# Attention and experts on one core: GpSimd's remainders of k and q as steps of their own, and a new written order

## The chip, the core and the metric

One core of a Trainium2 chip runs the whole program. The metric is the device time of one execution in microseconds (us). Three runs of the kernel before gave 1462.18, 1463.23 and 1466.3 us; the median, 1463.23 us, is the time to beat.

TensorE (PE) multiplies matrices, VectorE (DVE) and ScalarE (ACT) work on elements, GpSimd (POOL) does element work and gathers, SyncE (SP) issues transfers.

## What is computed

Attention over 8 batches and 8 heads of 576 positions with head dimension 64, where of each row of scores only those within tau of the row's maximum are kept; then a mixture of 8 experts with the best two of each token.

```python
scores = scale * np.matmul(q, k.transpose(0, 1, 3, 2))
thresh = np.max(scores, axis=-1, keepdims=True) - tau
scores = np.where(scores >= thresh, scores, -1000000000.0)
scores = scores - np.max(scores, axis=-1, keepdims=True)
attn = np.exp(scores)
attn = attn / (np.sum(attn, axis=-1, keepdims=True) + 1e-09)
return np.matmul(attn, v)
...
logits = x @ w_gate
noisy_logits = logits + np.log1p(np.exp(x @ w_noise)) * noise
top2 = np.argpartition(-noisy_logits, 2, axis=1)[:, :2]
...
h = np.maximum(x[mask] @ w1[e], 0.0)
out[mask] += top2_w[mask, k, None] * (h @ w2[e])
```

## The kernel before

The 64 pairs of batch and head are worked in 32 pairs of heads, n = 0 to 31 (four to a batch). Each pair has nine tiles of scores, j = 0 to 8, of 128 rows by 576 columns. For each tile PE computes the scores into PSUM (`scores`, L257 and, for j = 0, L262), DVE scales them into `ns` and takes the row's maximum (`rowmax`, L275), ACT computes `e` = exp (L277) and, once for two tiles, a threshold `thr` (L281), and DVE keeps what lies above it (`mask`, L303, one instruction with the two SBUF inputs ns and e). Then PE turns the masked tile (`ptile`, L320, L331, L334; `prem`, L348), ACT copies the result out of PSUM (L323, L337, L338, L351), PE multiplies with v (`avpiece`, `avrem`, L374), ACT copies the output (`oev`, L401), PE turns it for the gate (`xlpart`), and DVE scales it into `xr` (`xev`, L430 and L432), after `norm` (L361) and `invert` (L365, L366).

Scores are exact to float32 by three products of split operands. SP loads q and k of a pair in one transfer of 640 KB (`load`, L196, two buffers). `split_k` and `split_q` each let ACT round 128x640 elements to the short format (`hik`, `hiq`, L208) and then POOL compute the remainder (`lok`, `loq`, L209, 128x640, which reads the loaded tile and the rounded one in SBUF). hi and lo have two buffers each. Pair 0 uses the loaded values unsplit.

The order on every engine is written out by hand. `attention()` lists every step with a number, `at(g + t, step, n, ...)`, where g = 9n and t comes from the table PAIR (LAST for pair 31, NEXT for pair 30); the steps are sorted by that number and then issued, each to its engines. So a pair's steps reach over about two stretches of nine: in the steady state the last masks of one pair stand between the first steps of the next. An engine does its instructions in that order, and each waits until its inputs and buffers are ready.

Between these stand the steps of the gate of each finished batch (`gate_...`, small operations on DVE, ACT and POOL, and `gate_put`, L659 and L660, which POOL issues), and, from pair 30 on, the first steps of the experts: weights split by ACT and POOL (L838, L839), rows gathered by POOL (L886) and turned by DVE (L922) and POOL (L925). When attention is over, the experts run to the end of the program.

Of the kernel before, what the change touches and what calls it, by code (L numbers as in the profile page):

```python
# [10 lines left out]
F32 = mybir.dt.float32  # L11
# [5 lines left out]
ALU = mybir.AluOpType  # L17
# [37 lines left out]

NEXT = dict(
    scores=(-0.03, 1.15, 2.25, 3.09, 4.96), rowmax=(0.96, 1.61, 1.83, 2.74, 3.02, 3.28, 4.69, 5.12, 5.53),
    mask=(1.71, 2.04, 2.18, 4.54, 4.88, 5.36, 5.88, 5.87, 6.39), ptile=(7.71, 5.72, 7.01, 6.48, 7.05), prem=(8.49,),
    norm=(12.67,), invert=(15.81,), avrem=(10.66,), avpiece=(12.13, 13.04, 13.04, 13.69, 8.64, 8.65, 8.66, 11.21),
    oev=(14.72, 12.07), xlpart=(15.86, 15.72), xev=(16.20, 16.59))  # L60

MLAG = 2

# [10 lines left out]
    raw=(-19, -19, -9), tok=-27, ix=-24.5, ga=(-24, -22, -20), ba=(-22, -20, -18), la=(-20, -17, -15), ta=(-11, -10, -7),  # L74
# [78 lines left out]
def attention(tc, const, work, psum, state, qk, v, tau, wgn, noise, noise_r, out, x_dram, table, experts):  # L153
    nc = tc.nc
# [10 lines left out]
    def done(key):  # L165
        idle.append(used.pop(key))
# [14 lines left out]
    some, scale = (const.tile([128, 1], F32, name=x) for x in ("some", "scale"))  # L181
# [9 lines left out]
    raw = {}  # L191
# [36 lines left out]
    st = {}  # L228
# [61 lines left out]
    def mask(n, j):  # L290
        ns, thr, e = st.pop((n, j))
        t, s = tile_of(j)
        if j == 0:
            ssum[n] = rot(work, [128, 10], F32, name="ssum", bufs=3)
            pr = st["w", n] = rot(work, [128, S + 64], F32, name="pr")
            if n < 2:
                nc.vector.memset(pr[:, S:], 0.0)
            st["p", n, 8] = pr[:, None, 0:S]
        if s == 0:
            st["p", n, t] = P[:, next(turn) % 6]  # L300
        p = st["p", n, t][:, place(t, s) if j else 0, :]
# [102 lines left out]
    xr, xlp = {}, {}  # L404
# [38 lines left out]
    vec, gp = nc.vector, nc.gpsimd  # L443
# [225 lines left out]
    def at(g, f, *a):  # L669
        ev.append((g, len(ev), f, a))  # L670
# [10 lines left out]
    for n in range(NP):  # L681
        g = 9 * n
        d = dict(PAIR, **(LAST if n == NP - 1 else NEXT if n == NP - 2 else {}))
        for f in (scores, rowmax, mask):
            for i, t in enumerate(d[f.__name__]):
                at(g + t, f, n, 2 * i - 1 if f is scores and i else i)
        for i, t in enumerate(d["ptile"]):
            at(g + t, ptile, n, (i - 1) % 5)
        for f in (prem, norm, invert, avrem):
            at(g + d[f.__name__][0], f, n)  # L690
        for i, t in enumerate(d["avpiece"]):
            at(g + t, avpiece, n, i // 4, i % 4)
# [38 lines left out]
class Experts:  # L731
# [509 lines left out]
```

## Time and profile before

| | |
|---|---|
| median of three runs | 1463.23 us |
| profiled execution | 1465.06 us, of which the span in the trace 1463.2 us |
| PE busy | 1377.6 us (94%) |
| DVE busy | 918.8 us (63%) |
| ACT busy | 686.7 us (47%) |
| POOL busy | 598.1 us (41%) |

The times of the trace start with its span; the 1.86 us that the profiled execution took beside the span lie outside it. The shares are means over the whole program. Attention takes the span from 0 to about 600 us, the experts the rest, and the two have different limits, so each stretch is to be read by itself.

### The profile page before, as it was taken

Reading aid. Unit: us, or ns where it says so; the run is one execution under the profiler, and the core shown is the slowest. Engines: PE = TensorE matmul, PEld = TensorE weight load, DVE = VectorE, ACT = ScalarE, POOL = GpSimd, SP = SyncE. Lnnn points to the kernel's source line nnn. Section 1 sums busy time; section 2 is a strip of 40 time slices with the busy share of each in tenths; the row PEclk is TensorE's granted clock in tenths of the full one; section 3 lists DMA queues with packets and bytes.
Section 4 is the critical chain, followed back from the end, with each engine's and each line's share of the span. In section 5 each row is a group of like instructions: output and inputs, shape, how many; then the busy total and the mean of one; then the engine's idle time right before and its main releaser. Section 6 shows DMA issues by size and latency. Waiting matters only on the chain. (4 is left out here: it accounts for less than half of the span.)

```text
span 1463.2 us, 29503 instructions
## 1 busy us (share of the span) xinstructions
PE 1377.6 (94%) x11034; PEld 1166.2 (80%) x11034; DVE 918.8 (63%) x2558; ACT 686.7 (47%) x1447; POOL 598.1 (41%) x757
## 2 busy tenths in 40 slices
PE   8999999999999887889999999999999999999995
PEld 6667666766676555778988999999999989989884
DVE  8999999999999786453544444454454543543410
ACT  6888889898988776232222132232222221221210
POOL 2135555464746545533162262352432522521612
PEclk7999999999999887899999999999999999999998
DMA  5133425242414044455466376386375474573422
GB/s 174 61 110 91 136 85 147 67 135 67 135 45 124 21 121 119 81 132 107 149 151 158 80 167 153 87 183 152 83 186 136 115 169 110 133 172 83 69 30 32
DMA packets 154130, 166.55 MB, mean 114 GB/s; under 512 B 58148, under 2 KB 105340, under 8 KB 152960
## 3 DMA queue, kind: packets, MB, share of 16 engines
q1 hardware_dynamic: 126784, 125.21, 29.3%
q0 software_dynamic: 27200, 39.42, 16.2%
q8 instruction: 87, 1.43, 0.4%
q14 instruction: 59, 0.48, 0.1%
HBM read 104.42 MB, written 60.15 MB: 112 GB/s over the span
## 5 line engine op out<-in xcount | busy, mean ns | idle before, releaser
L303 DVE SCALAR_TENSOR_TENSOR p<-ns,thr,e 128x576 f32<-128x576 f32 x256 | 252.7, 1017 | 2.9 <-ACT thr L281 1.5
L277 ACT ACTIVATE e<-ns,nm 128x576 f32<-128x576 f32 x288 | 212.2, 779 | 45.3 <-DVE ns L275 44.4
L275 DVE TENSOR_SCALAR_CACHE_REDUCE ns<-sp 128x576 f32<-128x576 f32 x279 | 200.1, 746 | 31.7 <-PE sp L262 17.6
L374 PE MATMUL tp<-pt,vt 128*64 128x256 f32 (+1 forms) x1024 | 154.6, 435 | 1.2 <-ACT pt L323 0.9
L982 POOL DMA_INDIRECT out<-m_y,sx x43 | 68.1, 1585 | 206.9 <-DVE m_y L963 171.5
L257 PE MATMUL sp<-hik,hiq 64*128 64x288 f32 x496 | 124.0, 367 | 29.7 <-DVE ns L275 28.7
L982 POOL DMA_INDIRECT out<-m_y,ix x54 | 87.8, 1626 | 150.7 <-DVE m_y L1021 137.9
L323 ACT ACTIVATE pt<-tp 128x512 f32<-128x512 f32 x256 | 135.4, 596 | 24.9 <-PE tp L320 20.8
L963 DVE TENSOR_SCALAR m_y<-m_sp,gw 128x512 f32<-128x512 f32 (+1 forms) x43 | 32.3, 751 | 162.6 <-PE m_sp L961 162.6
L942 ACT ACTIVATE m_p<-m_tp 128x384 fp32r<-128x384 f32 (+1 forms) x66 | 32.6, 494 | 210.7 <-PE m_tp L940 210.6
L209 POOL TENSOR_TENSOR lok<-kq,hik 128x640 fp32r<-128x640 f32 x31 | 51.7, 1668 | 183.9 <-ACT hik L208 183.9
L257 PEld LDWEIGHTS sp<-hik,hiq 64*128 64x128 f32 x496 | 75.1, 207 | 56.3 <-DVE ns L275 51.0
L320 PE MATMUL tp<-ident,p 64*128 64x64 f32 x2048 | 107.2, 253 | 12.8 <-DVE xr L432 5.6
L320 PEld LDWEIGHTS tp<-ident,p 64*128 64x128 f32 x2048 | 98.4, 164 | 23.3 <-PE sp L257 10.3
L374 PEld LDWEIGHTS tp<-pt,vt 128*64 128x64 f32 x1024 | 67.5, 143 | 57.5 <-issue 24.1
L886 POOL DMA_INDIRECT m_p<-x_rows,sx x71 | 69.8, 983 | 92.7 <-DMA stage<-m_p 60.2
L257 PE MATMUL sp<-lok,hiq 64*128 64x288 f32 x496 | 104.6, 328 | 0.0
L660 POOL DMA_INDIRECT slot_table<-pay,sl x80 | 89.5, 1119 | 24.5 <-issue 12.7
L257 PE MATMUL sp<-hik,loq 64*128 64x288 f32 x496 | 98.6, 314 | 0.0
L942 ACT ACTIVATE m_hik<-m_tp 128x384 fp32r<-128x384 f32 (+1 forms) x11 | 5.6, 506 | 187.4 <-PE m_tp L940 187.4
L257 PEld LDWEIGHTS sp<-hik,loq 64*128 64x128 f32 x496 | 73.1, 209 | 0.0
L940 PE MATMUL m_tp<-m_pt,m_pt 128*128 128x384 f32 (+1 forms) x396 | 72.1, 340 | 0.0
(384 smaller groups left out, 3616.4 us busy)
## 6 DMA issues: line engine op xcount, KB each, us to landing
m_kq<-w SPq DMA_DIRECT2D x128, 256.0 KB
kq<-qk SPq DMA_DIRECT2D x32, 640.0 KB
stage<-m_p SPq DMA_DIRECT2D x63, 256.0 KB
vt<-v SPq DMA_DIRECT2D x8, 1280.0 KB
out<-zeros SPq DMA_DIRECT2D x19, 512.0 KB
x_rows<-xr SPq DMA_DIRECT2D x32, 256.0 KB
m_zeros<-stage SPq DMA_DIRECT2D x96, 64.0 KB
m_vt<-stage SPq DMA_DIRECT2D x96, 64.0 KB
```

Of the source, the lines that this page charges most:

```text
L209: nc.gpsimd.tensor_tensor(lo, x, hi.bitcast(F32), op=ALU.subtract)
L257: nc.tensor.matmul(sp[s][:, hh, 0:HALF], q_[p, 128 * t:128 * t + 128], k_[p, k0:k0 + HALF], start=(i == 0), stop=(i == last))
L275: nc.vector.tensor_scalar(ns, sp[:, :, 0:HALF], -1.0 / math.sqrt(D) if n else scale, None, op0=ALU.mult, op1=ALU.min, accum_out=nm)
L277: nc.scalar.activation(e, ns, AF.Exp, bias=nm, scale=-1.0)
L303: nc.vector.scalar_tensor_tensor(p, ns, thr, e, op0=ALU.is_le, op1=ALU.mult, accum_out=ssum[n][:, c:c + 1])
L320: nc.tensor.transpose(tp[a][:, 4 * s + kt, :], p[r, 128 * kt:128 * kt + 128], ident[r, r])
L323: nc.scalar.activation(pt[n][:, :, :, c:c + 64].rearrange("p s k c -> p (s k) c"), tp[a], AF.Copy)
L374: nc.tensor.matmul(av[n, i][64 * s:64 * s + 64, 0:PIECES[i][1] - PIECES[i][0]], w, x, start=(k == 1), stop=(k == 5))
L660: st = nc.gpsimd.indirect_dma_start(out=table, out_offset=bass.IndirectOffsetOnAxis(ap=d["sl"][0:m, i, c:c + 1], axis=0), in_=d["pay"][0:m ...
L886: self.nc.gpsimd.indirect_dma_start(out=r[0:m], out_offset=None, in_=x, in_offset=bass.IndirectOffsetOnAxis(ap=self.tok[e][2][0:m, t:t + 1 ...
L940: nc.tensor.matmul(ps[:, 0:n], w[:, 128 * c:128 * c + 128], x[:, c, 0:n], start=(i == 0), stop=(i == len(ops) - 1))
L982: st = self.nc.gpsimd.indirect_dma_start(out=out, out_offset=bass.IndirectOffsetOnAxis(ap=idx, axis=0), in_=y, in_offset=None, compute_op= ...
```

## The change

`split_k` and `split_q` now hold ACT's rounding alone. The subtraction on POOL is a step of its own, `split_rest`, with its own number in the table (`rest_k`, `rest_q`), and it gets a dependency on the DVE instruction (rowmax, mask or xev) that was issued last before it. All three tables have new numbers. `load(2)` moves from 5.54 to 8.76, and the puts of the last batches but one (`put0`) lie later and closer together. The same arithmetic is done as before.

```diff
 PAIR = dict(
-    scores=(-0.03, 1.15, 2.44, 3.28, 5.50), rowmax=(0.96, 1.91, 1.92, 3.22, 3.26, 4.63, 5.00, 7.40, 7.41),
+    scores=(1.09, 1.57, 2.27, 4.41, 8.72), rowmax=(1.45, 1.72, 1.82, 3.28, 3.30, 6.19, 7.12, 9.93, 10.27),
...
-    xev=(20.09, 20.43), split_q=(-9.93,), split_k=(-10.40,))
+    xev=(21.41, 21.02), split_q=(-9.01,), split_k=(-4.23,), rest_q=(-3.85,), rest_k=(-4.11,))
...
         nc.scalar.activation(hi, x, AF.Copy, scale=some)
-        nc.gpsimd.tensor_tensor(lo, x, hi.bitcast(F32), op=ALU.subtract)
         st[name, n] = hi, lo
+        st["raw", name, n] = x
+
+    def split_rest(n, name):
+
+        hi, lo = st[name, n]
+        sub = nc.gpsimd.tensor_tensor(lo, st.pop(("raw", name, n)), hi.bitcast(F32), op=ALU.subtract)
+        if "vec" in st:
+            tc.add_manual_dep(sub.ins, st["vec"].ins.name,
+                              mybir.DependencyInfo(mybir.DependencyClass.Sync, mybir.DependencyReason.DATA),
+                              reason="starts behind the last mask")
...
         if n + 2 < NP:
-            at(g - 3 if n else 5.54, load, n + 2)
+            at(g - 3 if n else 8.76, load, n + 2)
         if n:
...
+            at(g + (d["rest_q"][0] if n > 2 else max(d["rest_q"][0], -9.58)), split_rest, n, "q")
+            at(g + d["rest_k"][0], split_rest, n, "k")
```

**In the middle of the program.** GpSimd, in the fifth batch, before; lok and loq are the remainders, kq the loaded tile, L660 a put.

```order
L659 MEMSET spacer 1x1 [waits Pool_49]
L660 DMA slot_table<-pay_6334,sl_6342 37152x2
L209 TENSOR_TENSOR lok_6672<-kq_6340,hik_6671 128x640 [waits DMAHW5_49,PE_49,Activation_49]
L659 MEMSET spacer 1x1 [waits Pool_49]
L660 DMA slot_table<-pay_6334,sl_6342 37152x2
L209 TENSOR_TENSOR loq_6679<-kq_6340,hiq_6678 128x640 [waits PE_49,Activation_49]
L659 MEMSET spacer 1x1 [waits Pool_49]
```

VectorE at the same place before (ns to the right of the arrow: a mask; ns to its left: a row maximum; the numbers of tiles rise in the order of issue, so the step with hik_6671 was issued between the row maxima of ns_6664 and ns_6699):

```order
L275 TENSOR_SCALAR ns_6658,nm_6659<-sp_6613 128x576
L275 TENSOR_SCALAR ns_6664,nm_6659<-sp_6614 128x576
L303 SCALAR_TENSOR_TENSOR p,ssum_6472<-ns_6585,thr_6587,e_6589 128x576
L303 SCALAR_TENSOR_TENSOR p,ssum_6472<-ns_6593,thr_6587,e_6595 128x576
L275 TENSOR_SCALAR ns_6699,nm_6700<-sp_6682 128x576
L303 SCALAR_TENSOR_TENSOR p,ssum_6472<-ns_6658,thr_6660,e_6662 128x576
L303 SCALAR_TENSOR_TENSOR p,ssum_6472<-ns_6664,thr_6660,e_6666 128x576
L275 TENSOR_SCALAR ns_6764,nm_6765<-sp_6706 128x576
L275 TENSOR_SCALAR ns_6770,nm_6765<-sp_6707 128x576
L303 SCALAR_TENSOR_TENSOR pr_6779,ssum_6778<-ns_6699,thr_6701,e_6703 128x576
L430 TENSOR_TENSOR xr_120<-tp_6740,ssum_6141 128x4x80
L432 TENSOR_TENSOR xr_120<-tp_6740,ssum_6141 64x80
```

GpSimd after:

```order
L669 MEMSET spacer 1x1 [waits Pool_49]
L670 DMA slot_table<-pay_6301,sl_6310 37152x2
L217 TENSOR_TENSOR lok_6583<-kq_5947,hik_6582 128x640 [waits DVE_49,DMAHW3_49,PE_49,Activation_49]
L217 TENSOR_TENSOR loq_6356<-kq_5947,hiq_6355 128x640 [waits PE_49]
L669 MEMSET spacer 1x1 [waits Pool_49]
L670 DMA slot_table<-pay_6301,sl_6310 37152x2
```

VectorE after; the masks of ns_6485 and ns_6491 are the pair's second and third, and the remainders wait for the second:

```order
L313 SCALAR_TENSOR_TENSOR p,ssum_6519<-ns_6485,thr_6487,e_6489 128x576
L313 SCALAR_TENSOR_TENSOR p,ssum_6519<-ns_6491,thr_6487,e_6493 128x576
L285 TENSOR_SCALAR ns_6604,nm_6605<-sp_6568 128x576
L285 TENSOR_SCALAR ns_6615,nm_6605<-sp_6569 128x576
L313 SCALAR_TENSOR_TENSOR p,ssum_6519<-ns_6547,thr_6549,e_6551 128x576
L313 SCALAR_TENSOR_TENSOR p,ssum_6519<-ns_6553,thr_6549,e_6555 128x576
L313 SCALAR_TENSOR_TENSOR p,ssum_6519<-ns_6604,thr_6606,e_6608 128x576
L285 TENSOR_SCALAR ns_6672,nm_6673<-sp_6641 128x576
L285 TENSOR_SCALAR ns_6686,nm_6673<-sp_6642 128x576
L375 RECIPROCAL ssum_6190<-ssum_6190 64x1
L376 RECIPROCAL ssum_6190<-ssum_6190 128x9
L313 SCALAR_TENSOR_TENSOR p,ssum_6519<-ns_6615,thr_6606,e_6617 128x576
```

Before, the two remainders were issued with their roundings, next to the row maximum of j = 0 of the pair that follows, and needed only ACT. After, the two stand together, k first, and wait for the mask of ns_6485; the masks of ns_6547, ns_6553 and ns_6604 follow each other without a row maximum between.

**At the start.** ScalarE before: e_277 and e_281 are the last two exponentials of pair 0, hik_284 and hiq_289 the roundings of pair 2, which read the tile of the third load.

```order
L337 ACTIVATE pt_251<-tp_252 128x4x64 [waits PE_49]
L338 ACTIVATE ptr_265<-tp_252 64x64
L337 ACTIVATE pt_251<-tp_253 128x4x64 [waits PE_49]
L338 ACTIVATE ptr_265<-tp_253 64x64
L277 ACTIVATE e_277<-ns_273,nm_274 128x576 [waits DVE_49,Activation_49]
L277 ACTIVATE e_281<-ns_279,nm_274 128x576 [waits DVE_49,Activation_49]
L281 ACTIVATE thr_275<-nm_274,atau 128x2
L208 ACTIVATE hik_284<-kq_249,some 128x640 [waits DMAHW4_49]
L208 ACTIVATE hiq_289<-kq_249,some 128x640
L277 ACTIVATE e_305<-ns_301,nm_302 128x576 [waits DVE_49,Activation_49]
```

ScalarE after: e_281 and e_292 are now the last two exponentials of pair 0, hiq_272 the rounding of q of pair 2.

```order
L347 ACTIVATE pt_246<-tp_247 128x4x64 [waits PE_49]
L348 ACTIVATE ptr_260<-tp_247 64x64
L347 ACTIVATE pt_246<-tp_248 128x4x64 [waits PE_49]
L348 ACTIVATE ptr_260<-tp_248 64x64
L210 ACTIVATE hiq_272<-kq_270,some 128x640 [waits DMAHW5_49]
L287 ACTIVATE e_281<-ns_277,nm_278 128x576 [waits DVE_49,Activation_49]
L287 ACTIVATE e_292<-ns_290,nm_278 128x576 [waits DVE_49,Activation_49]
L291 ACTIVATE thr_279<-nm_278,atau 128x2
```

The rounding of q of pair 2, with its wait for the load (DMAHW), has moved ahead of pair 0's last two exponentials; that of k is issued later.

**Where attention ends.** TensorE before, ahead of the first scores of pair 31 (sp_10093): L348 is prem of pair 30, L374 with pt its product with v.

```order
L348 MATMUL tp_10073<-ident,p 128x64
L348 MATMUL tp_10074<-ident,p 128x64
L374 MATMUL tp_10086<-pt_9944,vt_8274 64x256 x6
L262 MATMUL sp_10093<-hik_9633,hiq_9641 128x288
L262 MATMUL sp_10093<-lok_9634,hiq_9641 128x288
```

TensorE after, at the same place: L330 is ptile of pair 30 (L320 before), sp_10102 the first scores of pair 31 (L272, L262 before).

```order
L330 MATMUL tp_10067<-ident,p 128x64
L330 MATMUL tp_10068<-ident,p 128x64
L272 MATMUL sp_10102<-hik_9890,hiq_9624 128x288
L272 MATMUL sp_10102<-lok_9891,hiq_9624 128x288
L272 MATMUL sp_10102<-hik_9890,loq_9625 128x288
```

Prem of pair 30 and its products with v, which stood ahead of pair 31's first scores, now stand behind them; two ptiles of pair 30 are left between its last mask and these scores.

## Rows read from the trace of the kernel before

**Rows 1.** The page: busy tenths of TensorE in 40 slices of the span.

```profile
PE   8999999999999887889999999999999999999995
```

**Rows 2.** Busy time in one stretch: length, engines (instructions), clock, DMA share, GB/s.

```profile
100.00:200.00 100.00, 92.61 (x1218) 68.42 (x1218) 97.62 (x286) 88.51 (x194) 54.11 (x76) 0.96 0.43 125
```

**Rows 3.** The page's groups: masks and row maxima (busy, mean ns | idle before).

```profile
L303 DVE SCALAR_TENSOR_TENSOR p<-ns,thr,e 128x576 f32<-128x576 f32 x256 | 252.7, 1017 | 2.9 <-ACT thr L281 1.5
...
L275 DVE TENSOR_SCALAR_CACHE_REDUCE ns<-sp 128x576 f32<-128x576 f32 x279 | 200.1, 746 | 31.7 <-PE sp L262 17.6
```

**Rows 4.** Timeline of SyncE's queue: loads of two pairs four apart.

```profile
318.25 0.33 SPq L196 DMA_DIRECT2D kq<-qk  x1
...
386.60 0.33 SPq L196 DMA_DIRECT2D kq<-qk  x1
```

**Rows 5.** Timeline of VectorE (start, duration, instruction), two places.

```profile
303.33 0.47 DVE L430 TENSOR_TENSOR xr<-tp,ssum 128x320 f32<-128x320 f32 x1
...
303.87 0.74 DVE L275 TENSOR_SCALAR_CACHE_REDUCE ns<-sp 128x576 f32<-128x576 f32 x1
...
304.55 0.74 DVE L275 TENSOR_SCALAR_CACHE_REDUCE ns<-sp 128x576 f32<-128x576 f32 x1
...
308.23 0.16 DVE L361 TENSOR_SCALAR ssum<-ssum 128x9 f32<-128x9 f32 x1
...
308.75 0.76 DVE L303 SCALAR_TENSOR_TENSOR p<-ns,thr,e 128x576 f32<-128x576 f32 x1
...
309.44 0.81 DVE L303 SCALAR_TENSOR_TENSOR p<-ns,thr,e 128x576 f32<-128x576 f32 x1
...
310.18 0.75 DVE L275 TENSOR_SCALAR_CACHE_REDUCE ns<-sp 128x576 f32<-128x576 f32 x1
...
331.21 1.55 DVE L303 SCALAR_TENSOR_TENSOR p<-ns,thr,e 128x576 f32<-128x576 f32 x1
...
332.69 2.08 DVE L303 SCALAR_TENSOR_TENSOR p<-ns,thr,e 128x576 f32<-128x576 f32 x1
```

**Rows 6.** Timeline of GpSimd around the same places.

```profile
314.02 2.17 POOL L209 TENSOR_TENSOR lok<-kq,hik 128x640 fp32r<-128x640 f32 x1 [0.80 <-ACT hik L208]
...
330.59 1.55 POOL L209 TENSOR_TENSOR lok<-kq,hik 128x640 fp32r<-128x640 f32 x1 [4.80 <-ACT hik L208]
332.10 2.06 POOL L209 TENSOR_TENSOR loq<-kq,hiq 128x640 fp32r<-128x640 f32 x1
```

**Rows 7.** Timeline of ScalarE: copies out of PSUM, exponentials, rounding.

```profile
304.26 2.06 ACT L323 ACTIVATE pt<-tp 128x512 f32<-128x512 f32 x4 [0.38 <-PE tp L320]
306.19 1.46 ACT L277 ACTIVATE e<-ns,nm 128x576 f32<-128x576 f32 x2
...
307.73 1.45 ACT L277 ACTIVATE e<-ns,nm 128x576 f32<-128x576 f32 x2
...
313.13 0.81 ACT L208 ACTIVATE hik<-kq,some 128x640 fp32r<-128x640 f32 x1
```

**Rows 8.** Timeline of ScalarE at the start.

```profile
20.48 1.44 ACT L277 ACTIVATE e<-ns,nm 128x576 f32<-128x576 f32 x2
...
22.94 0.83 ACT L208 ACTIVATE hik<-kq,some 128x640 fp32r<-128x640 f32 x1 [0.84 <-DMA kq<-qk]
```

**Rows 9.** Busy time from pair 30's first row maximum to pair 31's, and to attention's end.

```profile
529.40:566.60 37.20, 29.82 (x294) 20.10 (x297) 20.40 (x71) 21.82 (x46) 14.92 (x21) 0.68 0.36 114
566.60:601.50 34.90, 31.47 (x328) 22.07 (x329) 21.63 (x71) 19.65 (x44) 26.70 (x37) 0.85 0.48 108
```

**Rows 10.** Timeline of GpSimd, TensorE and VectorE ahead of pair 31's first row maximum.

```profile
547.43 1.29 POOL L839 TENSOR_TENSOR m_xr<-m_kq,m_xr 128x512 fp32r<-128x512 f32 x1 [9.32 <-ACT m_xr L838]
...
562.84 2.73 PE L374 MATMUL tp<-pt,vt 128*64 128x256 f32 x12 [0.38 <-ACT ptr L351]
565.50 0.40 PE L262 MATMUL sp<-hik,hiq 128*128 128x288 f32 x1
...
566.60 0.76 DVE L275 TENSOR_SCALAR_CACHE_REDUCE ns<-sp 128x576 f32<-128x576 f32 x1 [10.43 <-PE sp L262]
```

More of the change, by code (lines that the diff above doesn't have):

```diff
@@ L42 @@
 PAIR = dict(
-    scores=(-0.03, 1.15, 2.44, 3.28, 5.50), rowmax=(0.96, 1.91, 1.92, 3.22, 3.26, 4.63, 5.00, 7.40, 7.41),
-    mask=(2.08, 3.87, 3.96, 6.45, 7.07, 7.86, 9.37, 10.62, 10.77), ptile=(5.60, 11.42, 11.84, 10.20, 11.94),
-    prem=(14.02,), norm=(14.40,), invert=(14.94,), avrem=(18.05,),
-    avpiece=(12.69, 13.57, 14.01, 16.52, 14.63, 15.56, 15.72, 18.20), oev=(18.57, 18.24), xlpart=(19.61, 19.47),
-    xev=(20.09, 20.43), split_q=(-9.93,), split_k=(-10.40,))
+    scores=(1.09, 1.57, 2.27, 4.41, 8.72), rowmax=(1.45, 1.72, 1.82, 3.28, 3.30, 6.19, 7.12, 9.93, 10.27),
@@ L50 @@
+    mask=(2.35, 3.58, 6.12, 7.43, 9.84, 9.85, 10.39, 10.50, 10.59), ptile=(8.71, 10.28, 10.41, 10.65, 12.27),
+    prem=(14.74,), norm=(11.65,), invert=(19.36,), avrem=(17.85,),
+    avpiece=(12.46, 12.49, 13.00, 16.88, 15.48, 15.56, 18.09, 18.33), oev=(18.76, 19.08), xlpart=(19.62, 20.18),
+    xev=(21.41, 21.02), split_q=(-9.01,), split_k=(-4.23,), rest_q=(-3.85,), rest_k=(-4.11,))
 LAST = dict(
-    scores=(-0.03, 1.15, 2.17, 3.27, 4.43), rowmax=(0.96, 1.69, 1.75, 2.46, 2.85, 3.81, 3.93, 4.64, 5.61),
@@ L52 @@
-    mask=(1.90, 3.07, 3.17, 4.41, 4.53, 5.67, 5.69, 5.70, 6.49), ptile=(2.66, 4.36, 6.01, 6.45, 6.60), prem=(6.53,),
-    norm=(6.55,), invert=(8.30,), avrem=(6.96,), avpiece=(6.98, 7.19, 7.78, 7.78, 7.23, 7.31, 8.06, 8.26),
-    oev=(8.05, 8.48), xlpart=(8.30, 8.64), xev=(8.90, 8.97))
+    scores=(1.09, 1.57, 2.43, 3.75, 4.62), rowmax=(1.45, 1.62, 1.96, 3.16, 3.26, 4.09, 4.16, 4.78, 4.91),
+    mask=(2.76, 3.06, 3.92, 4.32, 4.54, 5.66, 6.83, 5.76, 5.92), ptile=(3.52, 4.31, 5.57, 7.50, 6.61), prem=(7.32,),
@@ L56 @@
+    norm=(7.25,), invert=(7.42,), avrem=(7.58,), avpiece=(6.62, 6.83, 7.46, 7.60, 7.67, 7.67, 7.71, 7.92),
+    oev=(8.05, 8.40), xlpart=(8.36, 8.61), xev=(8.90, 8.97))
 NEXT = dict(
-    scores=(-0.03, 1.15, 2.25, 3.09, 4.96), rowmax=(0.96, 1.61, 1.83, 2.74, 3.02, 3.28, 4.69, 5.12, 5.53),
-    mask=(1.71, 2.04, 2.18, 4.54, 4.88, 5.36, 5.88, 5.87, 6.39), ptile=(7.71, 5.72, 7.01, 6.48, 7.05), prem=(8.49,),
-    norm=(12.67,), invert=(15.81,), avrem=(10.66,), avpiece=(12.13, 13.04, 13.04, 13.69, 8.64, 8.65, 8.66, 11.21),
@@ L60 @@
-    oev=(14.72, 12.07), xlpart=(15.86, 15.72), xev=(16.20, 16.59))
+    scores=(1.09, 1.57, 2.15, 4.45, 6.58), rowmax=(1.45, 1.70, 1.90, 2.22, 3.72, 5.32, 6.48, 6.75, 7.56),
+    mask=(1.80, 4.83, 6.36, 4.77, 4.84, 7.19, 9.51, 8.84, 8.90), ptile=(4.45, 6.50, 8.05, 9.83, 9.90), prem=(10.33,),
+    norm=(12.91,), invert=(15.39,), avrem=(12.82,), avpiece=(12.05, 12.24, 12.34, 12.44, 13.68, 13.99, 14.20, 14.27),
+    oev=(12.92, 14.53), xlpart=(14.94, 15.24), xev=(15.96, 15.48))
 MLAG = 2
@@ L78 @@
     l2=(0.72, 0.74, 0.78, 0.82, 0.86, 0.9), eng=1,
-    put0=(-2.5, -2.25, -2, -1.75, -1.5, -1.25, -1, -0.75, -0.5, -0.25),
+    put0=(-1.5, -1.35, -1.2, -1.05, -0.9, -0.75, -0.6, -0.45, -0.3, -0.15),
     gate=(0.1, 0.11, 0.12, 0.13, 0.14, 0.15, 0.16, 0.17, 0.18, 0.3, 0.31, 0.32, 0.33, 0.34), put=(0.36,) * 10,
@@ L202, in load_values @@
         nc.sync.dma_start(raw["v", b], v[b])
+    st = {}
     def split(n, name, x):
@@ L226, in load_gates @@
                                   wgn[(2 * hp + s) * 64:(2 * hp + s + 1) * 64, :])
-    st = {}
     P = work.tile([128, 6, 2, S], F32, name="p", tag="p")
@@ L274, in rowmax @@
         nm, thr = (x[:, s or 0:(s or 0) + 1] for x in st["m", n, t])
-        nc.vector.tensor_scalar(ns, sp[:, :, 0:HALF], -1.0 / math.sqrt(D) if n else scale, None, op0=ALU.mult, op1=ALU.min, accum_out=nm)
+        st["vec"] = nc.vector.tensor_scalar(ns, sp[:, :, 0:HALF], -1.0 / math.sqrt(D) if n else scale, None, op0=ALU.mult, op1=ALU.min, accum_out=nm)
         e = rot(work, [128, 2, HALF], F32, name="e", bufs=MLAG + 2)
@@ L302, in mask @@
         c = 8 if j == 0 else 4 * s + t
-        nc.vector.scalar_tensor_tensor(p, ns, thr, e, op0=ALU.is_le, op1=ALU.mult,
+        st["vec"] = nc.vector.scalar_tensor_tensor(p, ns, thr, e, op0=ALU.is_le, op1=ALU.mult,
                                        accum_out=ssum[n][:, c:c + 1])
@@ L424, in xev @@
         b, hp = divmod(n, HP)
-        if (hp, s) == (0, 0):
+        if b not in xr:
             xr[b] = xrb[b % 2]
@@ L431, in xev @@
                                 r[:, 4 * s:4 * s + 4, None].to_broadcast([128, 4, 80]), op=ALU.mult)
-        nc.vector.tensor_tensor(xr[b][0:64, 4, h, :], ps[0:64, 320:400],
+        st["vec"] = nc.vector.tensor_tensor(xr[b][0:64, 4, h, :], ps[0:64, 320:400],
                                 r[0:64, 8 + s:9 + s].to_broadcast([64, 80]), op=ALU.mult)
```

## The prediction

> **What bounds the kernel now.** First the busy shares by slice and by stretch: they say where a change of order can act. TensorE is at nine tenths in the slices of the experts (the last 24 or so) [rows 1]; the change does not touch their work. In the middle of attention VectorE is busy 97.62 of 100 us, TensorE 92.61, ScalarE 88.51 [rows 2]: there a pair takes as long as VectorE needs, with ScalarE close behind. The loads of two pairs four apart start 318.25 and 386.60 us into the span [rows 4], so a pair takes 68.35 / 4 = 17.09 us. About 29 pairs run like that; the head and the last two pairs do not.
>
> Second the groups: what is VectorE busy with? A mask takes 1017 ns in the mean [rows 3], one that nothing disturbs 0.81 us, or 0.74 us from its start to the next instruction's at 309.44 and 310.18 [rows 5]. The excess is 256 x (1.017 - 0.81) = 53 us, or 53 / 32 = 1.66 us a pair. A row maximum keeps its 0.75 [rows 3].
>
> Third the timelines, for what stretches the masks. While the k remainder ran from 330.59 to 332.14 on GpSimd [rows 6], the mask at 331.21 took 1.55, and the next, beside the q remainder of 332.10, 2.08 [rows 5]: losses of 0.74 and 1.27, 2.0 together. A remainder that starts behind a mask under way takes 2.06 to 2.17 instead of 1.55 [rows 6]: it waits for that mask, then goes first, and the next mask waits for it. So mask and remainder exclude each other and take turns; a mask that becomes due inside a remainder loses what is left of it.
>
> Last the end of attention: from pair 30's first row maximum to pair 31's pass 37.20 us, with TensorE busy 29.82 at a granted clock of 0.68, half way between its two levels [rows 9]. VectorE stands idle 10.43 us until pair 31's first scores end [rows 10]. Ahead of these TensorE still does products of pair 30 from 562.84 [rows 10].
>
> **The change, part by part.** *Waits.* Both remainders now wait for the mask of j = 1. Behind them on GpSimd stand puts and the gate's small steps, which nothing in the pair waits for; the scores of the next pair need the remainders only some five microseconds later, when its first row maximum is due. The wait itself costs nothing where the rounding of k comes later than that mask; it does, as follows.
>
> *Where the k remainder falls.* I count from the start of rowmax 7, in the new order. VectorE: seven row maxima at 0.68 (303.87 to 304.55) [rows 5] = 4.76; six masks at 0.74 = 4.44; two xev at 0.54 (303.33 to 303.87) = 1.08; norm and the inverse 0.52 (308.23 to 308.75). The mask of j = 2 is done at 10.80, the two row maxima behind it at 12.16, and then mask 3 is due. ScalarE in its new order: its first exponential at 0.85 (0.74 of the row maximum and a tenth, an estimate); two exponentials and a threshold 1.54 (306.19 to 307.73) [rows 7] plus two output copies, 0.3 put for the one between them (an estimate); four copies 1.93 (304.26 to 306.19); half of 1.54 and a tenth for the lone exponential and its threshold, 0.87; two copies 0.97; 1.54; 0.97; 1.54; the rounding 0.81. That makes 11.32. So GpSimd starts the k remainder under rowmax 5 and ends it at 12.87, 0.71 after mask 3 is due.
>
> *What the pair then costs.* Mask 3 loses 0.71 at most, and less where a gate step or a short wait makes VectorE late. There is room for that: 17.09 less nine row maxima (6.12), nine masks (6.66), 1.08, 0.52 and the 1.66 of excess leaves 1.05 a pair of such things. I take the middle, 0.35. Mask 3 goes next, the q remainder takes its turn behind it, and mask 4, which stands directly behind mask 3, loses 1.27, as at 332.69. The sum is 1.62 against 1.66 before, 0.04 less: 29 x 0.04, rounded to -1.5 us. The bounds: 0.35 less a pair where the k remainder hides (-10), 0.35 more where mask 3 always loses all (+10). Nothing in the order makes the q remainder fall under the row maxima 7 and 8; before, it often did (314.02's successor), and that is what the change gives up.
>
> A rule that bears on this: the Trainium skill, SBUF — State Buffer, in the section on its two separate sides, says that the port pair shared by VectorE and GpSimd is an exclusive lock, held for a whole instruction by whichever starts first, for a VectorE operation with two SBUF inputs too. The rows agree on the exclusion (a mask of 2.08 beside a remainder of 2.06). It does not say who goes next when both wait.
>
> *The head.* Before, ScalarE did pair 0's last two exponentials at 20.48 and waited for the load until 22.94 [rows 8]. After, the rounding of q of pair 2 stands ahead of them, and its load still waits for pair 0's scores. So they start at about 22.94 + 0.83 = 23.8 instead of 20.48, 3.3 us late, and the masks and VectorE with them. ScalarE has one rounding less between (0.7), part of which comes back. I take +3; bounds 0 (if the later exponentials catch up, ScalarE being free at the start) and +4.
>
> *The end.* Of the 10.43 us of idle VectorE, prem's products go behind pair 31's first scores (2.73 from 562.84, and the prem and waits before it), and of the ptiles after the last mask two stay, with their copies. Two ptiles and the scores come to about 3 us (ptiles of 16 and 16 instructions, copies half of 1.93, scores 566.60 - 565.50 = 1.1). The gap would shrink by 7.4, and the rest of the reordered tables is worth about half a microsecond by the same reckoning: I take -8. But TensorE's work is only moved: it is busy 29.82 + 31.47 = 61.3 of 72.1 us [rows 9], so at most 10.8 can go. Bounds -12 (idle all gone, and the clock a little higher) and 0. *put0*, the gate's puts: GpSimd is busy 41% and not waited for by them; nothing, and if that cover were gone, the next pair's q remainder would be late, which is in the 0 of the end.
>
> **The sum.** -1.5 + 3 - 8 = -6.5 us against the profiled execution's 1465.06, so 1458.6. That execution was 1.83 above the median of the three runs; against the median 1463.23 it is 1456.7, in round numbers 1457.
>
> **Rivals.**
> 1. *The k remainder hides.* If ScalarE runs ahead by 0.5 us or more, the remainder is under way before mask 2 ends and done before mask 3 is due: 1.27 a pair instead of 1.66, 29 x -0.39 = -11, with +3 - 8: 1463 - 16 = 1447. For it: ScalarE is busy only 88.51 of 100 [rows 2]. Against: the chain above has no slack in it.
> 2. *Slower: two masks behind each other.* If the rounding comes 0.84 later than worked out, mask 3 has begun, the k remainder then holds mask 4 for 1.27 and the q remainder mask 5 for 1.27: 2.54 against 1.66, 29 x 0.88 = +26 if in all pairs, 1463 + 26 - 5 = 1484; in a half of them 1471. It decides from ScalarE at 12.16. For it: gate steps on ScalarE in each batch, and copies that wait for TensorE (0.38 before 304.26 [rows 7]). I price it at 1474.
> 3. *The end gives nothing.* The work moved behind pair 31's scores runs in its phase at the low clock, or GpSimd, which waited 9.32 us for a weight before [rows 10], holds the q remainder of pair 31 and with it the scores: 1463 - 1.5 + 3 = 1465, with half of the gain 1461. For it: 31.47 of 34.90 busy in that phase already [rows 9].
> 4. *VectorE keeps its turn.* If VectorE's masks, standing one behind the other, kept the port until row maximum 7, the q remainder would run under the two row maxima and mask 4 lose nothing: 29 x -1.27 = -37, 1420. Against: at 332.10 a waiting remainder went ahead of the next mask [rows 5, 6]. The lock as the Trainium skill tells it (SBUF — State Buffer, two separate sides) leaves room for this, since whoever starts first holds; no row of the trace shows it.
>
> **How the numbers follow.** Forecast 0.40 (its own range 1450 to 1461), rival 1 0.14, rival 2 0.22, rival 3 0.22, rival 4 0.02. A measurement of this kernel tells about 0.3%, 4.4 us, from no change. Faster by more than that, below 1458.8: three quarters of the forecast (0.30), rivals 1 and 4 (0.16), together 0.46. Slower: rival 2 (0.22) and a little of rival 3 (0.04), 0.26. Within: 0.28. The range takes the forecast, nearly all of rival 3 and the nearer parts of rivals 1 and 2: 1445 to 1475, which leaves out about 2 in 10.
>
> **What would show it.** In the trace after: loads four pairs apart by 4 x 17.05 = 68.2 us; the mean mask near 1.01 us, but with the long ones (2.0) all fourth masks and the half-long ones (about 1.1) third ones; the k remainder at 1.55 under rowmax 5, the q remainder at 2.0 beginning under mask 3; a 3 us gap of ScalarE near 20; the gap ahead of pair 31's first row maximum near 3 us, the stretch 529 to 601 some 8 shorter. It is wrong if the remainders hold two full masks a pair, if the q remainder starts elsewhere than behind mask 3, or if attention's end does not move with the gap.

## The result

The changed kernel took 1483.78 us (median of four runs, 1479.82 to 1490.42) against 1462.7 of the kernel before: 1.0146 of it, with an interval of 1.0103 to 1.0188. It is slower, and outside the range. Timed once more beside the experiments it came to 1.0106 (1.0089 to 1.0122). The profiled execution, the fastest of the four, has a span of 1478.1 us, 14.9 more than before; the other 6 of the 21 us between the medians lie in executions without a trace.

Of this span, pair 4 to pair 28 takes 76.5 to 507.2 us, and was 73.6 to 484.6; the last columns of the view are as in [rows 2]. First the stretches by window, after:

```profile
76.50:507.20 430.70, 357.70 (x4991) 271.06 (x4988) 380.06 (x1149) 356.62 (x788) 223.80 (x320) 0.96 0.34 99
...
552.40:581.70 29.30, 22.32 (x272) 16.49 (x272) 22.36 (x80) 21.37 (x45) 12.18 (x15) 0.85 0.38 121
581.70:615.80 34.10, 32.28 (x345) 24.43 (x345) 23.89 (x62) 19.58 (x44) 25.02 (x39) 0.88 0.42 110
```

and the middle before:

```profile
73.60:484.60 411.00, 380.05 (x4985) 283.18 (x4988) 399.55 (x1145) 361.01 (x787) 222.05 (x318) 0.95 0.35 102
```

The reader sees three things. In the middle, VectorE was busy 399.55 of 411.00 us and is busy 380.06 of 430.70: it works 19.5 us less, and stands idle 50.6 instead of 11.4 us. At the end, pair 30 to pair 31 takes 29.30 instead of 37.20 us [rows 9], and from pair 28's first row maximum to the last xev it is 615.8 - 507.2 = 108.6 where it was 601.5 - 484.6 = 116.9: 8.3 less. At the start pair 4 begins 2.9 us later. Together 2.9 + 19.7 - 8.3 = 14.3, nearly all of the 14.9.

What VectorE waits for in the middle, by the view of waits (us in total, times, longest), after (line numbers are 10 to 12 higher than before, those of the rounding and the remainder 2 and 8):

```profile
DVE p L313 <- ACT thr L291: 31.9, 6, 5.3
DVE gq L651 <- POOL gs L640: 12.7, 6, 2.1
DVE ns L285 <- PE sp L267: 3.5, 7, 0.6
```

and before:

```profile
DVE ns L275 <- PE sp L262: 5.0, 8, 0.8
...
DVE gq L641 <- POOL gs L630: 0.6, 3, 0.2
```

The first wait, 5.3 us six times, is new: a mask waits for a threshold from ScalarE, in one pair of four, the one in which a batch's gate begins. The second comes a pair or two later in the gate, six times 2.1 us. The masks themselves have become cheaper, as the page's group shows, which answers to [rows 3]:

```profile
L313 DVE SCALAR_TENSOR_TENSOR p<-ns,thr,e 128x576 f32<-128x576 f32 x256 | 237.9, 956 | 40.8 <-ACT thr L291 40.8
```

956 ns for 1017. So less is lost to the collisions, and more elsewhere. Where, the timelines of the pair in which a batch's gate begins show, GpSimd first, then ScalarE and VectorE:

```profile
315.83 2.12 POOL L543 TENSOR_TENSOR t<-xr 128x320 f32<-128x320 f32 x1 [6.89 <-DVE xr L442]
318.03 0.53 POOL L546 TENSOR_TENSOR t<-t 128x160 f32<-128x160 f32 x1
318.63 1.62 POOL L548 TENSOR_TENSOR lgs<-t 128x80 f32<-128x80 f32 x1
320.22 1.54 POOL L217 TENSOR_TENSOR lok<-kq,hik 128x640 fp32r<-128x640 f32 x1
321.72 1.53 POOL L217 TENSOR_TENSOR loq<-kq,hiq 128x640 fp32r<-128x640 f32 x1
323.22 0.37 POOL L556 TENSOR_SCALAR ab<-lgs 128x40 f32<-128x40 f32 x1
323.67 0.27 POOL L557 TENSOR_TENSOR ab<-ab,lgs 128x40 f32<-128x40 f32 x1
...
318.49 0.79 ACT L287 ACTIVATE e<-ns,nm 128x576 f32<-128x576 f32 x1
323.98 0.24 ACT L562 ACTIVATE ge<-ab 128x40 f32<-128x40 f32 x1 [4.69 <-POOL spacer L669]
...
325.37 0.82 DVE L313 SCALAR_TENSOR_TENSOR p<-ns,thr,e 128x576 f32<-128x576 f32 x1 [5.31 <-ACT thr L291]
```

GpSimd does the gate's sum (t, t, lgs; 315.83 to 320.25), then both remainders, which had been issued between the gate's steps, and only then ab, the input of the gate's exponential. On ScalarE this exponential (ge) stands behind the pair's sixth exponential (318.49), ahead of everything else that the pair needs: it waits 4.69 us, the next exponential and threshold wait behind it, and mask 5 starts 5.31 us late. (The timeline names the memset behind ab, L669, as what ended ScalarE's wait; in one of the six pairs the view of waits names ab itself, L557.) In the kernel before, ab follows the sum directly, and ge finds it ready four microseconds later; GpSimd, then ScalarE, before:

```profile
305.58 0.75 POOL L538 TENSOR_TENSOR lgs<-t 128x80 f32<-128x80 f32 x1
306.42 0.75 POOL L546 TENSOR_SCALAR ab<-lgs 128x40 f32<-128x40 f32 x1
307.25 0.27 POOL L547 TENSOR_TENSOR ab<-ab,lgs 128x40 f32<-128x40 f32 x1
...
311.20 0.24 ACT L552 ACTIVATE ge<-ab 128x40 f32<-128x40 f32 x1
```

The start and the end are as worked out; timelines after, of ScalarE and VectorE at the start and of VectorE ahead of pair 31:

```profile
24.89 0.83 ACT L210 ACTIVATE hiq<-kq,some 128x640 fp32r<-128x640 f32 x1 [6.50 <-DMA kq<-qk]
...
27.27 0.82 DVE L313 SCALAR_TENSOR_TENSOR p<-ns,thr,e 128x576 f32<-128x576 f32 x1 [3.77 <-ACT thr L291]
...
581.75 0.76 DVE L285 TENSOR_SCALAR_CACHE_REDUCE ns<-sp 128x576 f32<-128x576 f32 x1 [2.24 <-PE sp L272]
```

The rounding of q of pair 2 waits for its load to 24.89, mask 7 of pair 0 waits 3.77 for the exponentials behind it [rows 8]; and VectorE's idle time ahead of pair 31's first row maximum is 2.24 instead of 10.43 us [rows 10].

### The profile page after: what moved, and what is told of

Its sections match the earlier page's. It is cut to its first block, busy times and chain, and to the rows that moved or that the text cites. A ratio compares the mean times of both kernels' runs of the same rounds, so it can differ in the third digit from the quotient of the medians.

```text
span 1478.1 us, 29515 instructions
## 1 busy us (share of the span) xinstructions
PE 1344.5 (91%) x11034; PEld 1148.4 (78%) x11034; DVE 900.6 (61%) x2558; ACT 681.9 (46%) x1447; POOL 598.2 (40%) x757
## 5 line engine op out<-in xcount | busy, mean ns | idle before, releaser
L313 DVE SCALAR_TENSOR_TENSOR p<-ns,thr,e 128x576 f32<-128x576 f32 x256 | 237.9, 956 | 40.8 <-ACT thr L291 40.8
L384 PE MATMUL tp<-pt,vt 128*64 128x320 f32 (+1 forms) x1024 | 148.0, 420 | 3.6 <-issue 2.7
L267 PE MATMUL sp<-hik,hiq 64*128 64x288 f32 x496 | 109.5, 350 | 13.1 <-DVE ns L285 11.4
L330 PE MATMUL tp<-ident,p 64*128 64x64 f32 x2048 | 98.3, 241 | 8.4 <-ACT pt L333 4.0
L330 PEld LDWEIGHTS tp<-ident,p 64*128 64x128 f32 x2048 | 89.9, 154 | 19.6 <-ACT pt L333 6.4
L267 PE MATMUL sp<-lok,hiq 64*128 64x288 f32 x496 | 93.0, 309 | 0.0
L272 PE MATMUL sp<-hik,hiq 128*128 128x288 f32 x62 | 24.9, 401 | 74.4 <-DVE ns L285 74.4
L267 PEld LDWEIGHTS sp<-hik,hiq 64*128 64x128 f32 x496 | 66.4, 196 | 32.6 <-DVE ns L285 18.9
L267 PE MATMUL sp<-hik,loq 64*128 64x288 f32 x496 | 88.8, 300 | 0.0
L272 PEld LDWEIGHTS sp<-hik,hiq 128*128 128x128 f32 x62 | 13.8, 223 | 88.5 <-DVE ns L285 85.5
```

What stands on the lines that cost most here:

```text
L267: nc.tensor.matmul(sp[s][:, hh, 0:HALF], q_[p, 128 * t:128 * t + 128], k_[p, k0:k0 + HALF], start=(i == 0), stop=(i == last))
L272: nc.tensor.matmul(sp[0][:, hh, 0:HALF], q_[:, 512:640], k_[:, 64 + HALF * hh:64 + HALF * hh + HALF], start=(i == 0), stop=(i == last))
L313: st["vec"] = nc.vector.scalar_tensor_tensor(p, ns, thr, e, op0=ALU.is_le, op1=ALU.mult, accum_out=ssum[n][:, c:c + 1])
L330: nc.tensor.transpose(tp[a][:, 4 * s + kt, :], p[r, 128 * kt:128 * kt + 128], ident[r, r])
L384: nc.tensor.matmul(av[n, i][64 * s:64 * s + 64, 0:PIECES[i][1] - PIECES[i][0]], w, x, start=(k == 1), stop=(k == 5))
```

## The experiments

Theory: the place of the gate on GpSimd and ScalarE costs the time. Rivals: two masks held in each pair (rival 2 of the prediction, which had priced itself at just the time that came out); the added dependency; ScalarE too full in the new order.

Each ratio is to the kernel before as it was timed beside that run: 1463.18 us for the first four experiments, 1458.63 for the next four, 1458.87 for the last three. Times of different groups are therefore compared by their ratios.

**The gate's exponential later.** The changed kernel, in which ScalarE does the gate's exponential behind the pair's last two exponentials:

```diff
-GATING = (0, 1.6, 3.2, 4.6, 7.2, 7.3, ...
+GATING = (0, 1.6, 6.62, 6.9, 7.2, 7.3, ...
```

> The changed kernel, with the gate's exponential on ScalarE moved behind the pair's last exponential (3.2 to 6.62, and the step after it 4.6 to 6.9). Theory (one pair in four, the gate's exponential stands at the head of ScalarE's queue and waits for GpSimd, where the two remainders now stand ahead of its input; VectorE then waits 5.3 us for a threshold, six times 31.9 us in the stretch of whole batches): most of those 5.3 us go, 25 to 32 us in all, so 1452 to 1459. Rival (two masks held in every pair, the loss that I had priced at 0.9 us a pair): the time stays at 1480 to 1487. Rival (ScalarE is too full and the wait only moves to the next threshold): 1475 or more.

Measured: 1468.33 us, 1.0041 (1.0018 to 1.0064), that is 0.0065 to 0.0105 or 10 to 15 us less than the changed kernel in its two timings. The gain is less than the 25 to 32 us expected (1452 to 1459), and the time lies in neither rival's band, so both rivals fall. The wait for the threshold is gone; what came in its place, by VectorE's waits in pairs 4 to 28:

```profile
DVE gq L651 <- POOL gs L640: 13.3, 6, 2.3
DVE ns L285 <- PE sp L267: 9.0, 14, 1.2
DVE ns L285 <- remote: 3.9, 3, 1.4
...
DVE p L313 <- ACT thr L291: 0.5, 3, 0.2
```

and the page's group of the masks of that run:

```profile
L313 DVE SCALAR_TENSOR_TENSOR p<-ns,thr,e 128x576 f32<-128x576 f32 x256 | 244.8, 984 | 6.0 <-ACT thr L291 5.5
```

31.9 us have become 0.5, but TensorE's scores come later (9.0 for 3.5), and the masks take 984 ns: while VectorE stood still, the two remainders had run beside no mask (1.54 and 1.53 at 320.22 and 321.72), and now they hold masks again, 6.9 us of VectorE's time over the 256. In these pairs masks 5 and 6 take 1.50 and 1.28 us in the mean, where they took 0.82 and 0.76.

**And the gate's slots ahead of the remainder.** On top of it (below this is the second run):

```diff
-GATING = (0, 1.6, 6.62, 6.9, ... 15.5, 18.6, 19.3, 19.4, 21.2, 21.7)
+GATING = (0, 1.6, 6.62, 6.9, ... 15.5, 18.3, 18.9, 19.0, 21.2, 21.7)
```

> As the one before, and the gate's steps rank, base and slot a little earlier (18.6, 19.3, 19.4 to 18.3, 18.9, 19.0), so that GpSimd does them before the k remainder. Theory (VectorE waits 2.1 us, six times 12.7 us in all, for a product that GpSimd does behind the k remainder): 8 to 13 us less than the one before, 1440 to 1450. Rival (this wait is covered by another, or comes back as a later remainder): no difference to the one before, within 4 us.

Measured: 1464.24 us, 1.0007 (0.9991 to 1.0023), 5 us less than the one before by the ratios and 4 by the medians, less than the 8 to 13 expected. The two intervals overlap, so the times do not exclude the rival. In the trace, the wait for gs no longer stands among VectorE's waits, and the masks take 1006 ns, 5.7 us more in all. With both gate waits gone, the kernel stands where the kernel before stood, and its masks too (1006 and 1017 ns).

**The end alone.** The kernel before with the new tables LAST and NEXT and the new put0, nothing else:

```diff
-    scores=(-0.03, 1.15, 2.17, 3.27, 4.43), rowmax=(0.96, 1.69, ...
+    scores=(1.09, 1.57, 2.43, 3.75, 4.62), rowmax=(1.45, 1.62, ...
```

> The kernel before, with the changed kernel's tables for the last two pairs and for the puts at the end; the middle and the roundings with their remainders as before. Theory (the end gains 8 us by itself): 1453 to 1457. Rival (the gain at the end hangs on the late remainders of pairs 30 and 31): 1460 to 1466.

Measured: 1457.0 us, 0.9961 (0.9943 to 0.9978), 6 us less than before: the upper edge of the theory, and below the rival's band. From pair 30 to pair 31 it takes 31.10 us instead of 37.20:

```profile
528.60:559.70 31.10, 22.69 (x272) 16.34 (x274) 22.16 (x80) 21.05 (x45) 15.61 (x20) 0.84 0.40 129
559.70:593.40 33.70, 30.24 (x333) 21.27 (x334) 22.84 (x61) 19.52 (x43) 24.11 (x33) 0.90 0.41 112
```

Over both stretches TensorE is busy 22.69 + 30.24 = 52.93 us (605 records) where it was 61.3 (622 records) [rows 9], at clocks of 0.84 and 0.90 instead of 0.68 and 0.85. Counted from pair 28 on, so that steps moved from one stretch to the other drop out, it is 89.46 us (1027 records) for 96.49 (1030). Nearly the same work took less time, so the gain was not only in waits.

**The kernel before with the gate in that place.** The remainders and all else where they were; the gate's steps moved so that the remainders stand between the sum and ab, and ge right behind the roundings:

```diff
-GATING = (0, 1.6, 3.2, 4.6, 7.2, 7.3, ...
+GATING = (0, 5.47, 5.52, 7.17, 8.6, 8.7, ...
```

> The kernel before, with the gate's steps behind its sum moved so that the two remainders of a pair stand on GpSimd between the sum and the next step, and the gate's exponential on ScalarE right behind the roundings; nothing else is changed. Theory (this place of the gate is what costs in the changed kernel): ScalarE waits 4 to 5 us in one pair of four, seven batches, and VectorE 2 to 5 us for it: 15 to 30 us more than before, 1478 to 1493. Rival (the new order of the pair costs, not the gate): no change, 1460 to 1467.

Measured: 1496.05 us, 1.0226 (1.0202 to 1.025): 33 us slower than before, by the gate's place alone and a little more than expected; the rival falls. The view of ScalarE's waits:

```profile
ACT ge L552 <- POOL ab L547: 30.3, 6, 5.2
```

30.3 us in six batches, of the same kind as in the changed kernel. The masks also hold VectorE 6.5 us longer than before (259.2 for 252.7).

**Both remainders under row maxima.** What would the collisions be worth if the remainders fell where they hold nothing? On the second run's kernel:

```diff
-    xev=(21.41, 21.02), split_q=(-9.01,), split_k=(-4.23,), rest_q=(-3.85,), rest_k=(-4.11,))
+    xev=(21.41, 21.02), split_q=(-9.01,), split_k=(-5.74,), rest_q=(-8.14,), rest_k=(-2.87,))
...
+            at(g + (d["split_q"][0] if n != 2 else -7.68), split_q, n)
```

(load 0.2 later in the order, behind the k remainder; pair 31's k as before.)

> The changed kernel with the gate's steps as in the second run, and both remainders put where VectorE does row maxima: that of q behind the mask that precedes row maxima 7 and 8 (of the pair two earlier, right behind its rounding), that of k, with its rounding 1.5 earlier in the order, behind the mask that precedes row maxima 5 and 6; at the start the rounding of q of pair 2 behind pair 0's last two exponentials. Theory (masks lose what is left of a remainder when they become due, about 49 us over the second run, and a row maximum loses nothing): 0.2 us a pair stay for the k remainder, 1.2 to 1.4 a pair go where ScalarE and TensorE can follow: 20 to 40 us less than the second run, 3 of it from the start: 1425 to 1445. Rival (TensorE or ScalarE, 92 and 88 of 100 busy before, become the bound at once): 1450 to 1462. Rival (a remainder loses its turn to masks and is late for the scores): 1462 or more.

Measured: 1423.79 us, 0.9775 (0.9755 to 0.9795), 2.2% below the kernel before. By the ratios that is 34 us less than the second run, within the 20 to 40 expected, and both rivals fall.

**The dependency away.** The changed kernel without it:

```diff
-        if "vec" in st:
-            tc.add_manual_dep(sub.ins, st["vec"].ins.name,
```

> The changed kernel without the dependency of the remainders on VectorE; order on every engine as there. Theory (the rounding of k ends behind the mask that the remainders wait for, so the dependency holds nothing back): within 4 us of the changed kernel, 1480 to 1487. Rival (GpSimd is held by that wait in many pairs, and the gate behind it): 1475 or less. Rival (without the wait a remainder starts ahead of a mask and blocks one more): 1490 or more.

Measured: 1474.37 us, 1.0105 (1.0083 to 1.0126). The changed kernel has 1.0146 and 1.0106: beside the second no difference at all, beside the first the intervals overlap. (In us the run falls into the band of the rival, 1475 or less; but the changed kernel itself came to 1474.43 where it was timed again, so that band tells nothing.) The wait that the change adds costs nothing and gives nothing in this order, as far as 2 or 3 us can be told.

**The start mended.** The changed kernel with the rounding of q of pair 2 behind pair 0's last two exponentials:

```diff
-            at(g + (d["split_q"][0] if n > 2 else max(d["split_q"][0], -9.6)), split_q, n)
+            at(g + (d["split_q"][0] if n != 2 else -7.68), split_q, n)
```

> The changed kernel with the rounding of q of pair 2 behind pair 0's last two exponentials, else as there. Theory (ScalarE's wait for the load at the start costs 3.8 us of VectorE): 2 to 4 us less than the changed kernel. Rival (the lost time is made good by a later wait): no difference.

Measured: 1472.01 us, 1.0119 (1.0081 to 1.0157). The time cannot tell it from the changed kernel: the median lies 2.4 us below that of its second timing, the ratio 0.0013 above. The traces tell more: pair 4 begins at 74.0 us, and at 76.5 and 78.0 in the two profiles of the changed kernel.

**The q remainder alone.** On the second run's kernel:

```diff
-    xev=(21.41, 21.02), split_q=(-9.01,), split_k=(-4.23,), rest_q=(-3.85,), rest_k=(-4.11,))
+    xev=(21.41, 21.02), split_q=(-9.01,), split_k=(-4.23,), rest_q=(-8.14,), rest_k=(-4.11,))
```

> As the second run, with the q remainder alone moved behind the mask that precedes row maxima 7 and 8 of the pair two earlier. Theory (it no longer holds a mask; 1.27 us in 24 to 29 pairs, of which a part turns into waits for TensorE and ScalarE): 15 to 35 us less than the second run, 1430 to 1449. Rival (another engine bounds at once): 1455 to 1464.

Measured: 1422.01 us, 0.9742 (0.9723 to 0.9761), 37 us below the kernel before and by the ratios 39 below the second run (1.0007), a little more than the 15 to 35 expected; the rival falls. Pairs 4 to 28 take 459.1 - 73.0 = 386.1 us for 414.0. The page's group shows the masks:

```profile
L313 DVE SCALAR_TENSOR_TENSOR p<-ns,thr,e 128x576 f32<-128x576 f32 x256 | 227.4, 917 | 4.9 <-ACT thr L291 4.9
```

and the remainders' line (duration ns minimum/median/maximum):

```profile
L217 POOL TENSOR_TENSOR loq<-kq,hiq x31: 1537/1563/1585, 8.2 to 495.6; 128x640 fp32r<-128x640 f32 x31
L217 POOL TENSOR_TENSOR lok<-kq,hik x31: 1537/1561/2067, 16.0 to 510.4; 128x640 fp32r<-128x640 f32 x31
```

The q remainder's median is 1563 ns, where it was 2062 in the second run: it no longer waits for a mask. The masks take 917 ns instead of 1006, 23 us of VectorE's time over the 256. One wait of the gate is left: VectorE's reciprocal gr waits 7.0 us in all, five times, for GpSimd's gu.

**The same with the start mended, the changed kernel again, and the same without the dependency.**

```diff
-            at(g + (d["split_q"][0] if n > 2 else max(d["split_q"][0], -9.6)), split_q, n)
+            at(g + (d["split_q"][0] if n != 2 else -7.68), split_q, n)
...
+            at(g + (d["rest_q"][0] if n != 2 else -7.66), split_rest, n, "q")
```

> As the run with the q remainder alone behind the mask ahead of row maxima 7 and 8, and the rounding of q of pair 2 behind pair 0's last two exponentials. Theory (the start's wait is on the way to the end): 2 to 4 us less than that run, a ratio of 0.971 to 0.974 to the kernel before. Rival: the same as that run.

> The changed kernel as it is, beside the others on one chip, so that the runs without the dependency and with the start mended have a value to stand against. Theory: a ratio of 1.012 to 1.018 to the kernel before, 2 to 4 us above the run with the start mended and within 4 us of the run without the dependency. Rival (the dependency costs): 6 us or more above the run without it.

> As the run with the q remainder alone moved, without the dependency on VectorE. Theory (the rounding of q ends when the mask in question is over, so the dependency seldom holds): within 4 us of that run. Rival (there the wait is what keeps the remainder off the masks): 8 us or more above it.

Measured: 1418.03 us, 0.9719 (0.9703 to 0.9736), the fastest of all, and 2.8% below the kernel before; 1474.43, 1.0106 (1.0089 to 1.0122); and 1420.45, 0.9735 (0.9719 to 0.9751). The mended start gives 0.0023 here, 3 us as expected, though the intervals overlap; pair 4 begins at 67.8 us, and at 73.0 without it. The changed kernel comes a little below the 1.012 to 1.018 expected, 0.0001 from the run without the dependency, so the rival falls. The dependency does nothing here either, 0.9735 against 0.9742.

## Why the prediction was wrong

The step that failed is the sentence on the waits: behind the remainders "on GpSimd stand puts and the gate's small steps, which nothing in the pair waits for". One of them, ab, is what ScalarE's exponential of the gate waits for, and that stands in ScalarE's one queue ahead of the pair's own. The order of GpSimd that the prediction looked at shows only puts beside the remainders, and it counted ScalarE's chain for a pair without the gate. It asked what the remainders hold on VectorE, and for the gate only what GpSimd's time costs. Two waits, 31.9 and 12.7 us, came of it in the middle; the kernel before with the gate so placed loses 33 us, and the changed kernel with it mended stands level with the kernel before.

How the gate came behind the remainders stands in the two kernels, and not in the account of the change: its steps are numbered from the pair's last xev (`x = g + max(d["xev"])`), which moved from 20.43 to 21.41. With it ab moved from 22.33 to 23.31, past the remainders at 22.89 and 23.15, and gs from 40.13 to 41.11, past a later pair's k remainder at 40.89. At their numbers of before both would stand ahead of these remainders; no run tries it.

The other steps, by their own terms:

- *The middle without the gate*: -1.5 us forecast. In the second run, where both gate waits are gone, pairs 4 to 28 take 491.9 - 77.9 = 414.0 us against 411.0 before: +3, that is 0.12 a pair where -0.04 stood. Right as to size, but partly by luck. Masks 3 and 4 were to lose 0.35 and 1.27 a pair. Counted in these 24 pairs, mask 3 takes 1.42 and mask 4 1.55 in the mean, so they lose 0.61 and 0.74, and masks 5 and 6 lose 0.12 each: 1.59 a pair, where 1.62 stood. The k remainder starts under row maximum 6 in 12 pairs and under 5, as drawn, in 4; the q remainder starts beside mask 3 in 16. This profile is also among the fastest executions of that kernel (1458.22 for a median of 1464.24). The prediction says that before, the q remainder "often" fell under row maxima; it was short, under 1.75 us, in 8 of 31 pairs.
- *The mean mask* was to stay near 1.01 us and fell to 956 ns: in two of a batch's four pairs, remainders ran while VectorE stood still for the gate. In the second run it is 1006.
- *The start*: +3 forecast, 2.9 in the spans (4.4 in the second profile of the changed kernel), 3.77 of wait.
- *The end*: -8 forecast, -8.3 in the spans; alone, on the kernel before, 6 us. The size was right, the reason half: the prediction took TensorE's 61.3 us of work as fixed, and it was done in 22.32 + 32.28 = 54.6. The 0.68 that it calls half way between the clock's two levels is a mean of 0.5 and 1.0 in the records (1.2 and 2.4 GHz), and nearer the lower.
- *Rival 2* gave 1484 for two held masks in all pairs, and the time came to 1483.78. That is chance. In one pair of four, the first of a batch, two masks are held (1.72 and 2.09 us in the mean), but over pairs 4 to 28 the masks lose 1.07 a pair, for 1.87 before by the same count, where the rival needed 2.54. It rested on a rounding 0.84 late, and what came was a wait of 4.69 in one pair of four.
- *The dependency*, which the prediction put at nothing, is nothing.

The exclusion of mask and remainder held in all thirteen traces, and with it the Trainium skill's lock (SBUF — State Buffer, two separate sides): no mask under 1.0 us stands beside a remainder under 1.75 us for more than 0.4 us. The run with the q remainder under row maxima, which read PSUM, got its duration down to 1563 ns, and 23 us of mask time with it; the 53 row maxima that share over 0.5 us with a remainder took 0.75 us in the mean, like the others (745 ns). The 1.27 a pair for the q remainder, 37 us in 29 pairs, which the prediction worked out in rival 4, are there to be had: moving it gave 1.0007 to 0.9742, some 39 us, of which 28 lie between pairs 4 and 28, and 24 of these are VectorE's busy time (371.54 for 395.50). It did not move by itself, as that rival would have had it.

Why the run with both remainders moved is no better than with q alone (0.9775 and 0.9742, masks at 953 and 917 ns; the intervals overlap) the traces show in the gate's pair. The k remainder has the later number there (-2.87 for -4.11; only its rounding comes earlier, and it ended 7 us before), so that ab and a put go ahead of it on GpSimd. It starts beside mask 6, and the q remainder behind it beside mask 7. Both remainders moved, GpSimd and VectorE:

```profile
292.35 1.55 POOL L217 TENSOR_TENSOR lok<-kq,hik 128x640 fp32r<-128x640 f32 x1
...
292.19 2.33 DVE L313 SCALAR_TENSOR_TENSOR p<-ns,thr,e 128x576 f32<-128x576 f32 x1
...
295.60 1.99 DVE L313 SCALAR_TENSOR_TENSOR p<-ns,thr,e 128x576 f32<-128x576 f32 x1
```

With q alone, the same pair; the k remainder starts behind mask 5 and runs under row maxima, and mask 6 keeps its 0.76:

```profile
292.55 2.06 POOL L217 TENSOR_TENSOR lok<-kq,hik 128x640 fp32r<-128x640 f32 x1
...
294.92 0.76 DVE L313 SCALAR_TENSOR_TENSOR p<-ns,thr,e 128x576 f32<-128x576 f32 x1
```

The end's gain does not need a higher granted clock, as the second profile of the changed kernel shows. From pair 28 to the last xev, before and there:

```profile
484.60:601.50 116.90, 96.49 (x1030) 67.68 (x1026) 77.62 (x241) 71.76 (x155) 66.13 (x90) 0.80 0.36 94
...
509.30:616.10 106.80, 90.25 (x1003) 66.58 (x1000) 78.79 (x242) 70.49 (x154) 61.94 (x85) 0.81 0.37 103
```

10.1 us less at 0.81 against 0.80. Open is how much the clock adds in the profiles in which it is higher.

## What to carry to other kernels

Where an instruction is moved on a queue, list what stands behind it there, who waits for that, and what stands behind the waiter on its own queue, for the rare pair in which other work begins too: here steps of 0.37 and 0.27 us on GpSimd came late, ScalarE stood 4.69 us and VectorE 5.31. Look also at what is counted from a number that moves: here the gate, from xev. A mended wait is worth its length less what it had been covering: 45 us of waits gave 15 to 20, mainly since remainders that had run beside an idle VectorE held masks again (250.5 us of masks for 237.9), and VectorE's waits for TensorE's results grew from 3.5 to 12.9 us. Work that excludes one kind of instruction belongs beside another: the same subtraction held a mask for 1.27 us and a row maximum not at all.

## What the runs showed of the hardware

The granted clock of one stretch differs between executions of the same kernel: from pair 30 to pair 31 the changed kernel shows 0.85 in one profile and 0.71 in the other, and the stretch takes 29.30 and 32.30 us. So the rise from 0.68 before to 0.85, or to 0.84 with the end alone, cannot be read as the effect of the order: the eleven traces with the new end lie between 0.71 and 0.85, the two with the old one at 0.68 and 0.74. Which is cause and which effect no run tells.
